# Matmuls on a constant tile, placed in TensorE's early waits, in a linear-attention kernel with a feed-forward block

## The chip, the cores and the metric

The kernel runs on one core of a Trainium2 chip. A core has a matrix engine (TensorE, PE in the profile, with its weight loads shown as PEld), a vector engine (VectorE, DVE), a scalar engine (ScalarE, ACT), a general engine (GpSimd, POOL) and an engine that mainly issues transfers (SyncE, SP). SBUF is the on-chip memory that the engines work in; PSUM holds the results of matmuls, here in eight banks. Each engine takes its instructions in order, and they wait for one another by semaphores.

The metric is the device time of one execution in microseconds. The number given for a kernel is the median of its runs.

## The reference

For 8 batches of 8 heads, with 576 rows of 64 elements, the attention part computes a kernelized attention with 128 random features; its output, 4608 rows of 512, goes through a feed-forward block of 2048 hidden elements.

```python
def phi(x):
    proj = np.einsum('bhsd,md->bhsm', x, omega)
    sq = np.sum(x * x, axis=-1, keepdims=True) / 2.0
    h = proj - sq
    h = h - np.max(h, axis=-1, keepdims=True)
    return np.exp(h) / np.sqrt(m)
q_p, k_p = (phi(q_s), phi(k_s))            # q and k scaled by 64 ** -0.25
kv = np.einsum('bhsm,bhsd->bhmd', k_p, v)
z = np.sum(k_p, axis=2)
num = np.einsum('bhsm,bhmd->bhsd', q_p, kv)
den = np.einsum('bhsm,bhm->bhs', q_p, z)[..., None] + 1e-06
x = (num / den)                            # to rows of 8 heads * 64
h = x @ w_in
g = h * np.clip(h + 3.0, 0.0, 6.0) / 6.0
out = g @ w_out
```

The constants of `phi` that depend on a row alone cancel between numerator and denominator for q; for k the maximum is divided out of v (`cc`, the reciprocal of `mx`).

## The kernel before

The program is written as a list of operations, and a planner in the kernel's own code puts them in order when the program is built. Each operation (`op`) has the engines that may run it, a cost in microseconds, a priority (lower goes first), the keys that it reads and writes, and, for a matmul, the PSUM bank that it needs (`alloc`; the eight banks are the `ring`, and a `Virt` is a bank not yet chosen). `Prog.schedule` (L102) keeps one clock for each engine. In each step it looks, for every engine, at the operations whose predecessors have been placed, takes the one that can start first (or a more urgent one that can start almost as soon), and over all engines places the earliest. A matmul takes the bank that has been free longest; `slot_of` finds it. Transfers share a modelled bandwidth (`flow`). `Prog.emit` then writes each engine's instructions in the order found, with a semaphore wait wherever an operation depends on one of another engine that is not yet known to be done. The order is thus fixed at build time; only the waits are decided on the chip.

The work of a batch is `attention(b)`:

- `load` brings q, k and v. For batch 0, SP and ACT issue float32 transfers (L467), which are cast on the chip (`cast`, evicted through the helper at L389 to L393). From batch 1 on, POOL issues q and k with a cast in the transfer.
- `turns` transposes k and q on PE (L405 for batch 0, L406 later) and copies the result to `kT` and `qT`.
- The K matmuls (L606) multiply with omega, 128 by 256 columns each, two to an operation; ACT exponentiates them to `kp` (L612) and DVE takes the maximum (L615). `project` does the same for q (L623 on PE, L627 on ACT).
- `pair` makes, for two heads, `cc` (L707), the scaled v (`vc`, L711 and L716), the product kv (L724, L726), its copy `kvz`, the numerators (L747), the division (L759, L763) and the transposition of the result to `xT` (`turn_x`). Batch 0 does this in two halves, "A" and "B".

The feed-forward block of a batch follows one batch behind: `mm1_half` (L840) for batch 0, in two halves of 256 rows, `mm1` (L815) later, and `mm2` (L870) one further behind. Their matmuls are the dense part of the run.

What starts the transfers matters for the change. At the start SP issues omega (L412), k and q, the remaining rows of k, and v. POOL issues the four pieces of w_in (L443) behind the landing of v of batch 0 (`W_GATE`). k of batch 1 waits for the third piece of w_in, q of batch 1 for the fourth:

```python
    W_GATE = [("v32", 0, 1), ("v32", 0, 3), ("v32", 1, 3), ("v32", 1, 3)]
...
            load(1, (), {"k": [("wi", 2)], "q": [("wi", 3)], "v": [("kb", 1, 16)]})
```

The first instructions of PE are one matmul that makes omega's transposed copies (L428, behind two casts on DVE, with two copies by DVE after it, L431 and L433), then the transposes of k of batch 0.

Of the kernel before, what the change touches and what calls it, by code (L numbers as in the profile page):

```python
# [5 lines left out]
BF16 = mybir.dt.bfloat16  # L6
# [4 lines left out]


URGENT = 0.5
EV0 = (("ACT","DVE"), ("ACT","DVE"), ("POOL","DVE"), {"k": ("POOL", "ACT", "DVE"), "q": ("POOL", "ACT","DVE")})


# [24 lines left out]
class Prog:  # L41
# [60 lines left out]
    def schedule(self):  # L102
        for o in self.ops:
            o.ndep = len(o.deps)
            for d in o.deps:
                d.succ.append(o)
        engines = {}
        for o in self.ops:
            for e in o.engs:
                engines.setdefault(e, [])  # L110
        free = {e: 0.75 for e in engines}
        queues = {}
        clock = [0.0]

        def flow(until, keep):

            now, qs = clock[0], {q: [list(x) for x in l] for q, l in queues.items()}
            while True:
                heads = [l for l in qs.values() if l and l[0][2] <= now + 1e-9]
                later = [l[0][2] for l in qs.values() if l and l[0][2] > now + 1e-9]  # L120
                if not heads and not later:
                    break
                if not heads:
                    step = min(later) - now
                    if now + step >= until:
                        break
                    now += step
                    continue
                total = sum(l[0][0].packet for l in heads)
                step = min([l[0][1] * total / l[0][0].packet for l in heads] + [x - now for x in later] +  # L130
                           [until - now])
                now += step
                for l in heads:
                    l[0][1] -= step * l[0][0].packet / total
                    if l[0][1] <= 1e-9:
                        l[0][0].end = now
                        l.pop(0)
                if now >= until - 1e-9:
                    break
            if keep:  # L140
                clock[0] = max(until, clock[0])
                queues.update(qs)

        def ready(o):
            return max(o.ready, max([d.end + d.lat + o.slack for d in o.late])) if o.late else o.ready

        def add(o):
            o.ready = max([d.end + (0.0 if d.eng == "PE" and o.engs == ("PE",) else d.lat + o.slack)
                           for d in o.deps if d.group is None] + [0.0])
            o.late = [d for d in o.deps if d.group is not None]  # L150
            for e in o.engs:
                engines[e].append(o)

        for o in self.ops:
            if o.ndep == 0:
                add(o)
        order = []
        n = len(self.ops)

        def slot_of(o):  # L160
            t, picks = 0.0, []
            for vx in o.alloc:
                idle = sorted((0.0 if h is None else h.free_at, i) for i, h in enumerate(vx.ring.held)
                              if h is None or h.left == 0)
                if len(idle) <= o.spare:
                    return None
                t = max(t, idle[o.spare][0])
                picks.append(idle[0][1])
            return t, picks

        while len(order) < n:
            best = None
            for e, lst in engines.items():
                cand = []
                for o in lst:
                    s = slot_of(o) if o.alloc else (0.0, ())
                    if s is None:
                        continue
                    cand.append((max(free[e], ready(o), s[0]), o, s[1]))
                if not cand:  # L180
                    continue
                m = min(x[0] for x in cand)
                c = min((x for x in cand if x[0] <= m + (URGENT if x[1].prio < -1.0 else 0.02)),
                        key=lambda x: (x[1].prio, x[1].seq))
                if best is None or c[0] < best[0]:
                    best = (c[0], e, c[1], c[2])
            if best is None:
                raise RuntimeError("stuck: " + str([(e, [o.name for o in l][:5]) for e, l in engines.items()]))
            st, e, o, picks = best
            for x in o.engs:  # L190
                engines[x].remove(o)
            o.eng = e
            occ = o.occ[e] if isinstance(o.occ, dict) else o.occ
            for vx, i in zip(o.alloc, picks):
                old = vx.ring.held[i]
                if old is not None:
                    for d in old.users:
                        o.deps.setdefault(d, False)
                vx.slot = i
                vx.ring.held[i] = vx  # L200
            o.start = st
            if o.group is not None:
                free[e] = st + o.issue
                flow(free[e], True)
                queues.setdefault(e, []).append([o, occ, free[e]])
                flow(1e9, False)
            else:
                free[e] = st + occ
                o.end = free[e]
            for vx in o.virts:  # L210
                vx.left -= 1
                vx.free_at = max(vx.free_at, o.end + o.lat)
            order.append(o)
            for s in o.succ:
                s.ndep -= 1
                if s.ndep == 0:
                    add(s)
        self.order = order
        return order
# [79 lines left out]
def _emit(nc, es, q, k, v, omega, w_in, w_out, out):  # L299
# [20 lines left out]
    alpha = float(D) ** -0.25  # L320
    PE_T, PE_X = 2, 2
    SPARE = 1
    EV_T = ("DVE", "ACT")
    EV_C = ("POOL", "ACT", "DVE")
    EV_V = ("POOL", "DVE")
    EV_L = ("POOL", "ACT")
    K0, T0, V0, C0 = EV0
    EV_K = ("DVE", "ACT")
    EV_O = ("ACT", "DVE")

    def sbt(name, shape, dt):
        return es.enter_context(nc.sbuf_tensor(name, list(shape), dt))
# [5 lines left out]
    q32 = sbt("q32", [128, NCH, D], F32)  # L338
# [22 lines left out]
    osb = [sbt("osb%d" % u, [128, HID], F32) for u in range(4)]  # L361
    wi = sbt("wi", [128, NJ, DFF], BF16)
    wo = sbt("wo", [128, NF, HID], BF16)
    om32 = sbt("om32", [M, D], F32)
    om2 = sbt("om2", [M, 2, D], BF16)
    om = sbt("om", [128, 2, M], BF16)
# [4 lines left out]
    ring = Ring([P8[:, i, :] for i in range(8)])  # L371
# [3 lines left out]
    op = G.op  # L375
# [10 lines left out]
    def both(n, fast=1):  # L386
        return {"ACT": actt(n), "DVE": 0.07 + n / 960.0 / fast}
# [36 lines left out]
    for i in range(2):  # L424
        op("DVE", 0.15, lambda E, i=i: E.tensor_copy(om2[:, i, :], om32[:]), -9, reads=["om32"],
           writes=[("om2", i)])
    vom = Virt(ring)
    op("PE", 0.1, lambda E: E.matmul(ring.t[vom.slot][:, 0:M], om2[:].rearrange("m t d -> m (t d)"), ident[:],  # L428
                                     start=True, stop=True),
       -9, reads=[("om2", 0), ("om2", 1), "ident"], writes=[vom], alloc=[vom], lat=0.25)  # L430
    op("DVE", 0.2, lambda E: E.tensor_copy(om[0:64, 0, :], ring.t[vom.slot][0:64, 0:M]), -9, reads=[vom],  # L431
       writes=["om0"])
    op("DVE", 0.2, lambda E: E.tensor_copy(om[64:128, 1, :], ring.t[vom.slot][64:128, 0:M]), -9, reads=[vom],  # L433
       writes=["om1"])
    omk = ["om0", "om1", "omz0", "omz1"]


    WI = [(0, 4), (4, 8), (8, 12), (12, 16)]
# [73 lines left out]
    def attention(b):  # L512
        pb = b % 2
        sl = 0.0 if b == 0 else 1.0
        sp = 0 if b == 0 else SPARE

# [26 lines left out]
        def turns(t, name, dbl, dst, src, p):  # L543
# [3 lines left out]
            def e_T(E):  # L547
# [5 lines left out]
               writes=[vT], alloc=[vT], lat=0.25, slack=sl, spare=sp, name="T%s%d.%s" % (t, b, name))  # L553
            op(EV_T if b else T0, both(n, 1 if b else 2), evac(lambda: dst, lambda: turned(vT, b, n).rearrange(
                "p (j t) -> p j t", j=dst.shape[1])),
# [143 lines left out]
    def pair(b, m, t):  # L699
        pb = b % 2  # L700
        sl = 0.0 if b == 0 else 1.0
        sp = 0 if b == 0 else SPARE
        u2 = (b * NP + m) % 2
# [184 lines left out]
    for b in range(B):  # L888
        if b == 0:
            load(0, ("SP", "ACT", "SP", "ACT"), {t: [] for t in "kqv"})  # L890
            for i in range(len(WI)):
                w_in_piece(i, [W_GATE[i]])
        elif b == 1:
            load(1, (), {"k": [("wi", 2)], "q": [("wi", 3)], "v": [("kb", 1, 16)]})
            for g, key in enumerate((("qb", 1, 16),("qb", 1, 16),("qb", 1, 16),("qb", 1, 16))):
                w_out_piece(g, [key])
        elif b == 2:
            load(2, (), {"k": [("wo", 2)], "q": [("wo", 3)], "v": [("wo", 3)]})
        else:
            load(b, (), {"k": [("m1", b - 2, 6)], "q": [("m1", b - 2, 9)], "v": [("m1", b - 2, 15)]})  # L900
        attention(b)
        if b == 0:
            continue
        blk = b - 1
        if blk == 0:
            for half in range(2):
                for f in range(0, NF, 2):
                    mm1_half(half, f)
            continue
        for f in range(NF):  # L910
            mm1(blk, f)
            if f % 4 == 0:
                mm2(blk - 1, f // 4)
# [47 lines left out]
```

## Time and profile before

| | us |
|---|---|
| median of 5 runs | 331.83 |
| the five runs | 329.91, 331.05, 331.83, 332.25, 332.53 |
| the profiled execution: its time | 330.35 |
| the profiled execution: its span | 328.5 |

A profile is taken of one execution. Its span runs from the first instruction to the last; 1.85 us of that execution's time lie around it.

| engine | busy us | share of the span | instructions |
|---|---|---|---|
| PE | 313.1 | 95% | 2185 |
| DVE | 209.5 | 64% | 455 |
| ACT | 193.6 | 59% | 393 |
| POOL | 77.5 | 24% | 109 |

Busy time is an average over the whole run; the change touches only the first stretch of it. There the engines look as follows (busy time of each engine in stretches from the start of the span):

| stretch, us | PE | DVE | ACT | POOL |
|---|---|---|---|---|
| 5 to 6 | 0.53 | 0.41 | 0.55 | 0.00 |
| 8 to 9 | 1.00 | 1.00 | 0.86 | 0.94 |
| 11 to 12 | 0.97 | 0.42 | 1.00 | 0.60 |
| 12 to 13 | 0.26 | 1.00 | 1.00 | 0.79 |
| 13 to 14 | 0.26 | 0.97 | 1.00 | 0.93 |
| 15 to 16 | 0.53 | 0.97 | 0.48 | 0.87 |
| 18 to 19 | 0.70 | 0.91 | 0.78 | 0.70 |
| 22 to 23 | 1.00 | 0.06 | 0.36 | 0.00 |
| 29 to 30 | 0.21 | 1.00 | 0.92 | 0.68 |
| 30 to 31 | 0.40 | 0.70 | 0.00 | 0.00 |

PE waits longest, in order of time, before its first matmul (3.37 us), before the first transposes of k (1.82 us, at 5.47), before the q projections (1.48 us, at 13.74, for ACT's copy of qT), before the first kv (0.64 us, at 15.47), and before the transposes of k of batch 1 at 30.07. In the profile, "idle before" is the time for which an engine had nothing running ahead of an instruction, and the name behind the arrow is what released it. The ends of matmuls are modelled, and matmuls overlap, so the rate of PE is better read from start to start of many equal ones than from the length of one.

### The profile page before, as it was taken

Reading aid. Unit: us, or ns where it says so; the run is one execution under the profiler, and the core shown is the slowest. Engines: PE = TensorE matmul, PEld = TensorE weight load, DVE = VectorE, ACT = ScalarE, POOL = GpSimd, SP = SyncE. Lnnn points to the kernel's source line nnn. Section 1 sums busy time; section 2 is a strip of 40 time slices with the busy share of each in tenths; the row PEclk is TensorE's granted clock in tenths of the full one; section 3 lists DMA queues with packets and bytes.
Section 4 is the critical chain, followed back from the end, with each engine's and each line's share of the span. In section 5 each row is a group of like instructions: output and inputs, shape, how many; then the busy total and the mean of one; then the engine's idle time right before and its main releaser. Section 6 shows DMA issues by size and latency. Waiting matters only on the chain.

```text
span 328.5 us, 5726 instructions
## 1 busy us (share of the span) xinstructions
PE 313.1 (95%) x2185; PEld 168.6 (51%) x2185; DVE 209.5 (64%) x455; ACT 193.6 (59%) x393; POOL 77.5 (24%) x109
## 2 busy tenths in 40 slices
PE   3788999999999999999999999999999999999994
PEld 2466774555545554555555555555555444444442
DVE  4868896599777757875687577856775433443311
ACT  3877992389369546764776477646764444344400
POOL 2815527037034402240235023502110000000000
PEclk9999999999999999999999999999999999999999
DMA  7999999969993996799569963997022111000033
GB/s 257 240 184 149 228 181 144 254 167 154 208 199 44 161 198 193 89 159 188 191 79 148 190 208 38 154 210 225 10 56 60 39 50 48 33 32 34 34 86 72
DMA packets 89355, 44.32 MB, mean 135 GB/s; under 512 B 56048, under 2 KB 84720, under 8 KB 89328
## 3 DMA queue, kind: packets, MB, share of 16 engines
q1 hardware_dynamic: 62272, 30.98, 40.7%
q0 software_dynamic: 26512, 12.46, 31.2%
q10 hardware_dynamic: 544, 0.52, 0.5%
q8 instruction: 17, 0.28, 0.4%
q14 instruction: 10, 0.08, 0.1%
HBM read 36.73 MB, written 9.44 MB: 141 GB/s over the span
## 4 chain that ended last, share of the span: by engine, by line
PE 86%; DMA 8%; POOL 1%; ACT 1%; issue 1%; SPq 1%; DVE 0%; POOLq 0%
PE p L870 37%; PE p L815 34%; PE p L623 4%; PE p L606 3%; DMA wi<-in_moe_w_in_dram 3%; PE p L747 3%; PE p L724 2%; DMA xT<-xb 2%; PE p L840 2%; DMA q<-in_q_dram 2%; DMA k<-in_k_dram 1%; PE p L406 1%; SPq L467 1%; POOL wi L443 1%; PE p L726 0%
## 5 line engine op out<-in xcount | busy, mean ns | idle before, releaser
L870 PE MATMUL p<-wo,gT 128*128 128x512 bf16 x576 | 142.8, 379 | 0.0
L823 DVE SCALAR_TENSOR_TENSOR gT<-tsb,p 128x512 bf16<-128x512 bf16 x128 | 87.4, 686 | 68.0 <-ACT tsb L821 67.6
L821 ACT ACTIVATE tsb<-p 128x512 bf16<-128x512 f32 x128 | 76.8, 602 | 69.6 <-PE p L815 68.3
L815 PE MATMUL p<-xT,wi 128*128 128x512 bf16 x448 | 111.6, 379 | 0.5 <-DMA xT<-xb 0.5
L870 PEld LDWEIGHTS p<-wo,gT 128*128 128x128 bf16 x576 | 55.3, 98 | 55.9
L815 PEld LDWEIGHTS p<-xT,wi 128*128 128x128 bf16 x448 | 42.9, 98 | 46.3 <-DMA xT<-xb 1.0
L612 ACT ACTIVATE kp<-p 128x512 bf16<-128x512 f32 x72 | 42.1, 609 | 24.7 <-PE p L606 24.4
L615 DVE TENSOR_REDUCE mx<-kp 128x4 f32<-128x512 bf16 x72 | 47.9, 678 | 11.4 <-ACT kp L612 11.0
L627 ACT ACTIVATE qpT<-p 128x512 bf16<-128x512 f32 (+1 forms) x80 | 43.1, 570 | 4.4 <-PE p L623 4.4
L711 POOL TENSOR_TENSOR vc<-v,cc 128x512 bf16<-128x512 f32 x24 | 25.1, 1047 | 46.9 <-DVE cc L707 26.8
L763 DVE TENSOR_TENSOR xb<-p,rec 128x384 bf16<-128x384 f32 (+1 forms) x64 | 28.4, 477 | 0.0
L606 PE MATMUL p<-om,kT 128*128 128x256 bf16 x144 | 26.5, 285 | 0.1
L623 PE MATMUL p<-qT,om 128*128 128x512 bf16 (+1 forms) x80 | 25.1, 358 | 1.5 <-ACT qT L392 1.5
L392 ACT COPY osb<-p 128x512 f32<-128x512 f32 x30 | 17.6, 588 | 6.7 <-PE p L870 6.3
L606 PEld LDWEIGHTS p<-om,kT 128*128 128x128 bf16 x144 | 13.5, 101 | 10.6 <-DVE kT L393 0.7
L646 POOL TENSOR_TENSOR vcl<-vl,cc 64x260 bf16<-64x260 f32 x6 | 3.7, 616 | 60.8 <-DMA vl<-in_v_dram 35.1
L747 PEld LDWEIGHTS p<-kvz,qpT 128*128 128x128 bf16 x312 | 13.9, 98 | 7.2 <-DVE kvz L393 0.6
L815 PE MATMUL p<-xS,wi 128*128 128x512 bf16 x64 | 16.4, 379 | 0.0
L840 PE MATMUL p<-xT,wi 128*128 128x256 bf16 x128 | 15.6, 273 | 0.2 <-ACT xT L392 0.2
L724 PEld LDWEIGHTS p<-vc,kp 128*128 128x128 bf16 x256 | 11.8, 98 | 7.8 <-DVE vcl L646 1.1
L747 PE MATMUL p<-kvz,qpT 128*128 128x65 bf16 x312 | 15.3, 194 | 0.6 <-DVE kvz L393 0.3
L724 PE MATMUL p<-vc,kp 128*128 128x65 bf16 x256 | 13.5, 194 | 1.6 <-DVE vcl L646 0.6
(71 smaller groups left out, 200.2 us busy)
## 6 DMA issues: line engine op xcount, KB each, us to landing
out_dram<-osb SPq DMA_DIRECT2D x32, 256.0 KB, 3.7
v<-in_v_dram SPq DMA_DIRECT2D x14, 512.0 KB, 5.4
wi<-in_moe_w_in_dram POOLq DMA_DIRECT2D x4, 512.0 KB, 9.3
k<-in_k_dram POOLq DMA_DIRECT2D x8, 256.0 KB, 4.5
k<-in_q_dram POOLq DMA_DIRECT2D x8, 256.0 KB, 5.6
wo<-in_moe_w_out_dram POOLq DMA_DIRECT2D x4, 512.0 KB, 10.1
kb<-in_k_dram POOLq DMA_DIRECT2D x6, 256.0 KB, 4.4
qb<-in_q_dram POOLq DMA_DIRECT2D x6, 256.0 KB, 7.2
```

Of the source, the lines that this page charges most:

```text
L606: ins = E.matmul(ring.t[vK.slot][:, 256 * i:256 * i + 256], kT[:, 2 * u + i, :], om[:].rearrange("d t m -> d (t m)"), start=True, stop=True)
L612: op("ACT", actt(512), lambda E, u=u, vK=vK: E.activation(kp[pb][:, 4 * u:4 * u + 4, :].rearrange("p c m -> p (c m)"), ring.t[vK.slot], AF ...
L615: op("DVE", dvet(512), lambda E, u=u: E.reduce_max(mx[pb][:, 4 * u:4 * u + 4], kp[pb][:, 4 * u:4 * u + 4, :], axis=AX.X), pos(u) + 0.03, r ...
L623: op("PE", mmt(n), lambda E, vQ=vQ, lh=lh: E.matmul(ring.t[vQ.slot][:, 0:n], om[:, lh, :], src, start=True, stop=True), p + 0.045 * lh, re ...
L627: op("ACT", actt(n), lambda E, vQ=vQ, lh=lh: E.activation(dst(lh), ring.t[vQ.slot][:, 0:n].rearrange("m (j t) -> m j t", t=128), AF.Exp, s ...
L724: E.matmul(o[:, 65 * hh:65 * hh + 65], kp[pb][:, c0 + i, :], vc[u2][:, 65 * i:65 * i + 65], start=(i == 0), stop=False)
L747: ins = E.matmul(d[:, hh, i - i0, :], qpT[pb][:, o:o + 128], kvz[m][:, 65 * hh:65 * hh + 65], start=True, stop=True)
L763: op("DVE", dvet(128 * n), lambda E: E.tensor_tensor(xv[:, :, i0:i1, :], psum()[:, :, :, 0:64], rbc, ALU.mult), t + 0.01, reads=[vn, ("rec ...
L815: ins = E.matmul(ring.t[vh.slot], wi[:, c, 128 * f:128 * f + 128], xv[:, c, :], start=(c == 0), stop=(c == NJ - 1))
L821: op("ACT", actt(512), lambda E: E.activation(tsb[tu][:], ring.t[vh.slot], AF.Relu, bias=0.5, scale=1.0 / 6.0), t - 0.1, reads=[vh], write ...
L823: op("DVE", dvet(512), lambda E: E.scalar_tensor_tensor(gT[gu][:, f, :], tsb[tu][:], 1.0, ring.t[vh.slot], ALU.min, ALU.mult), t - 0.1, re ...
L870: ins = E.matmul(ring.t[vo.slot], gT[gu][:, f, 128 * tc:128 * tc + 128], wo[:, f, :], start=(f == 0), stop=(f == NF - 1))
```

## The change

A tile `fill` of 128 by 384 bf16 is set to one by DVE at the start. Forty operations named "idle" are added for PE, each one matmul of 128 columns of `fill` (the weights) on 256 others. Each takes a PSUM bank; nobody reads what it writes. Sixteen of them depend on `fill` alone and have a cost of 0.22 us in the plan; 24 also depend on the last of q's main rows of batch 0 and have a cost of 0.11 us. They have the lowest priority, and the planner treats them apart: it takes the first idle operation only if it would end before the earliest other operation that PE could start, and only up to 21 us of its clock. When nothing but idle operations is left, the planner stops, and any that were not placed are not written.

```diff
+IDLE_UNTIL = 21.0
...
-                m = min(x[0] for x in cand)
+                idle = [x for x in cand if x[1].name == "idle"]
+                cand = [x for x in cand if x[1].name != "idle"]
+                m = min([x[0] for x in cand] + [1e9])
+                if idle and (not cand or idle[0][0] + idle[0][1].occ <= m):
+                    if idle[0][0] > IDLE_UNTIL:
+                        if not cand:
+                            continue
+                    elif best is None or idle[0][0] < best[0]:
+                        best = (idle[0][0], e, idle[0][1], idle[0][2])
+                        continue
+                    else:
+                        continue
+                if not cand:
+                    continue
...
+            if best is None and all(o.name == "idle" for l in engines.values() for o in l):
+                break
...
+    IDLE = (16, 24)
...
+    fill = sbt("fill", [128, 384], BF16)
...
+    op("DVE", 0.2, lambda E: E.memset(fill[:], 1.0), -9.5, writes=["fill"])
+
+    def idle_work(count, each, gate):
+        for i in range(count):
+            vw = Virt(ring)
+            op("PE", each, lambda E, vw=vw: E.matmul(ring.t[vw.slot][:, 0:256], fill[:, 0:128], fill[:, 128:384],
+                                                     start=True, stop=True),
+               9, reads=["fill"] + gate, writes=[vw], alloc=[vw], lat=0.0, name="idle")
...
+        if b == 0:
+            idle_work(IDLE[0], 0.22, [])
+            idle_work(IDLE[1], 0.11, [("q32", 1, 3)])
         attention(b)
```

## The prediction

> **What bounds the kernel now.** First the page: PE is busy 313.1 of 328.5 us, and the chain of waits is 86% PE. So a gain must either shorten PE's dense work or let it start sooner. The change adds 40 matmuls and removes none, so only the second is open. Next the waits of PE over the whole span: of 10.8 us, all but 1.1 us (0.55 at 50.19 us, 0.49 at 94.81 us) lie before 33.1 us. The question is thus what ends the early waits, and PE's timeline there shows it (columns: start, us, engine, line, operation, tiles, count, idle before with releaser):
>
> ```profile
> 5.47 1.03 PE L405 MATMUL p<-ident,kb 128*128 128x128 bf16 x8 [1.82 <-DVE kb L393]
> ...
> 8.28 1.91 PE L606 MATMUL p<-om,kT 128*128 128x256 bf16 x8
> 9.99 0.63 PE L405 MATMUL p<-ident,qb 128*128 128x128 bf16 x4
> 10.41 0.32 PE L405 MATMUL p<-ident,kb 128*128 128x128 bf16 x2
> 10.57 1.02 PE L606 MATMUL p<-om,kT 128*128 128x256 bf16 x6
> 11.43 0.83 PE L405 MATMUL p<-ident,qb 128*128 128x128 bf16 x12
> ...
> 30.07 0.40 PE L406 MATMUL p<-ident,k 128*128 128x128 bf16 x4 [0.85 <-DMA k<-in_k_dram]
> 31.01 0.27 PE L406 MATMUL p<-ident,k 128*128 128x128 bf16 x2 [0.55 <-DMA k<-in_k_dram]
> ```
>
> The last two rows are the point of this case: PE has finished all it can do for batch 0 and stands 0.85 + 0.55 = 1.40 us for k of batch 1. The chain of waits, asked for 0 to 36 us, says why k comes no sooner (start, us, what):
>
> ```profile
> 13.76 10.42 DMA wi<-in_moe_w_in_dram
> 24.18 0.29 issue
> 24.47 1.53 POOL k L467 x2
> 26.00 4.88 DMA k<-in_k_dram
> 30.88 0.14 issue
> 31.01 0.29 PE p L406 x2
> ```
>
> No PE work stands in it from 0 to 31 us. k of batch 1 is issued by POOL when the third piece of w_in (L443) has landed, those pieces when v of batch 0 has landed, and v when SP has worked through its queue. The second finding is a slow start of PE. The instructions of L606 from 5 to 9 us, and from 10.9 to 11.5 us (ns min/median/max):
>
> ```profile
> L606 PE MATMUL p<-om,kT x8: 394/421/421, 6.6 to 8.9; 128*128 128x256 bf16 x8
> ```
> ```profile
> L606 PE MATMUL p<-om,kT x5: 272/273/283, 10.7 to 11.3; 128*128 128x256 bf16 x5
> ```
>
> The same matmul falls from 421 to 273 ns at about 10.5 us, although the row of granted clock reads 1.00 in every microsecond from 0 to 34. Start to start it is (1.91 - 0.421)/7 = 0.213 us early and, from the 42 matmuls of L840 in 4.75 us at 21.57, (4.75 - 0.273)/41 = 0.109 us later. PE runs at half rate up to 10.5 us, and full from then on: the 65-column matmuls of L724 and L747 show 192 to 204 ns throughout 15 to 20 us.
>
> **The change part by part.** *The constant tile.* One DVE memset of 128x384 bf16. Between the 64x64 memset (0.11 us) and the 128x260 uint32 one (0.28), both rows of DVE; I take the upper, as the size in bytes is nearer to it. DVE idles 1.33 us before omega's cast at 3.01, so it costs nothing; without that cover, 0.28.
>
> *Where the 40 fillers go.* A filler is planned only where it ends before PE's next known work, so the order of the real work is kept. The planner's clock, worked from the costs in the code, agrees with the trace (k's transposes 30.01 planned, 30.07 measured); I use it only to place them. The first 16, at 0.22 each: 12 ahead of omega's matmul (planned 1.15 to 3.79), 4 behind it. The 24 gated on q (planned landing 9.17; the last casts of q start on the chip at 9.31 after a landing at 9.04): 2 behind q's first transposes, 2 ahead of the last K matmuls, 10 in the wait for qT (13.74, 1.48 us), 6 ahead of the first kv (15.47, 0.64 us), 3 and 1 in the next two waits (0.25 and 0.28 us).
>
> *Cost of the first 16.* 12 x 0.213 = 2.56 us from about 1.1 us on (DVE's first memset starts at 0.81, plus 0.28): they end near 3.7, and omega's matmul moves from 3.37 to 3.7. Its two copies (3.69 to 4.28) move 0.3 us into DVE's idle 0.70 us ahead of 4.99. The other 4 take 0.85 us, to 4.9 at the latest, inside the wait that k's cast ends at 5.47. Sum 0. Gone the cover, it would be 0.3 us at the first K matmul.
>
> *What they bring.* PE is now active from 1.1 us instead of 5.47. If it is at full rate by 7 us, the work from 7.43 to 10.5 takes half. What is late next is ACT: its idle after 7 us is only 0.24 us before 7.24, some 0.14 us around 8.8 and 0.24 us ahead of 10.77, then it is full to 15.2. From above: at full rate already at 5.47, the first exponential (ACT, idle 1.17 us before 7.24) comes about 0.5 us sooner too. So the batch-0 chain comes forward 0.4 to 0.9 us at most.
>
> *Cost of the 24.* Two and two go where the trace has no gap (9.99 to 12.2 is solid): 4 x 0.109 = 0.44 us, or 0.85 at half rate. The 10, the 6 and the 4 need 1.09, 0.65 and 0.44 us against waits of 1.48, 0.64 and 0.53: hidden within 0.01. A filler also waits for the readers of the PSUM bank it takes; no row shows such waits. Between 0 (the bank planned free is free; it can't be a gain) and the whole next wait, I take 0, since all banks around 12.7 to 13.8 are freed by ACT's exponentials (trace: done at 13.20), ahead of the qT copies that PE awaits there anyway.
>
> *Sum.* At the first mm1 (20.79) between 0.9 us sooner and 0.44 later. Either way it runs into the 1.40 us wait for k at 30.88. Does PE reach the chain that lands k? One place: POOL's `vc` (L716, 12.35) stands in its queue between the first and second w_in issue, and hangs on cc, done by DVE at 10.21. That is 2.1 us of slack, and before cc only the first 16 fillers stand. So k stays, and behind it ACT (kT, xT, qpT in a row from 31.32) and PE keep their order; 0.21 us of PE's wait at 33.07 (ACT xT, queued behind kT) can't move much. Sum on the profiled execution: 328.5 of span + 1.85 around it = 330.35, change -0.1, within +-0.3. The runs' median lies 1.48 above that execution. I carry the -0.1 to the median: **331.7 us**.
>
> **A rule weighed.** The Trainium skill, TensorE: Matmul & The Clock Gate, Part 1, says that half rate is the default, that about 3.4 us of sustained work lifts it, counted in a free-running window. Trace: 5.47 to 10.5 is 5.0 us. By its penalty rule (time throttled times one half) 5.0/2 = 2.5 us are to be had: 329.3. By the trace, where the time goes into the 1.40 us wait, nothing: 331.7. The measured wait decides. Against the 24, the same page ("HAM oscillation") has the clock fall only after a PE gap of over some 3.4 us; the longest wait after 5.47 here is 1.48 us, and the trace indeed shows no second fall. By this rule the 24 protect nothing; but it also lets the phase differ from run to run, which one trace can't exclude.
>
> **The rivals.** *A: no change* as above, 331.7. Chance 0.52.
>
> *B: the median run is slower than the profiled one because its clock rises late or falls again.* PE is busy only 26% from 12 to 14 us and about half in 15 to 17. Half rate over 32 matmuls of mm1 (3.4 us) adds 32 x 0.104 = 3.3 us; less the slack of 1.40 it leaves 1.9, just what lies between the lowest run (329.91) and the median. The fillers then bring the median to about **330.0** (330.35 and 329.91 are what good executions show). For it: five runs spread over 2.6 us. Against: the one trace shows no such fall, and transfers vary too. Chance 0.28.
>
> *C: the fillers overrun the waits.* PE takes them in order; if the array stays at half rate among them, 24 x 0.213 = 5.1 us stand in waits of 1.48 + 0.64 + 0.53 = 2.65, 2.45 too long; less 1.40 that the wait for k takes up, +1.1: **332.9**. At each one's whole 421 ns, with nothing overlapped, 10.1 - 2.65 - 1.40 = +6.1: 337.9, the upper end. I price it by the start-to-start row. It decides from 1.40 us of delay on. Against: L840's spacing shows full rate at that time. Chance 0.20.
>
> *D: the fillers don't lift the clock*, since constants might not count as activity: nothing moves at the end, so D is within A.
>
> **How the numbers follow.** I call 0.5% (1.7 us) what a measurement of this kernel can tell from no change. A: 0.02 faster, 0.47 same, 0.03 slower, for the spread of medians. B: 0.23 faster, 0.05 same (330.0 is 0.55% down, close to the bound). C: 0.11 slower by its upper part, 0.09 same. Sums: 0.25, 0.61, 0.14. A's own range is 330.9 to 332.5 (the spread of medians). The range goes down to 329.8 for all of B but an edge, and up to 333.5, which takes the lower half of C; what is left out is C's upper half (0.10) and edges of the others.
>
> **What would show it.** Right: L606 at 273 ns well before 10.5 us, mm1's first matmul moved by under 1 us, and PE's wait for k at 30 us longer by just as much, with k still landing near 30.9. A fall of 421 ns rows that reaches the end would need k to land sooner, which would make me wrong. C shows as mm1 starting after 22.2 us and no wait left before k's transposes; a changed moment of the w_in issues would break the argument at its root. B can't be seen in one trace, only in the spread of the runs: it would fall below that of before.

## The result, and the profile after

| | before | after |
|---|---|---|
| median of all runs taken side by side, us | 330.66 (79 runs) | 330.07 (44 runs) |
| lowest to highest, us | 328.59 to 333.75 | 328.86 to 333.03 |
| profiled execution: time and span, us | 330.35 and 328.5 | 329.53 and 327.7 |

The ratio after to before is 0.999, with a 95% interval of 0.9977 to 1.0004: no change that can be told from none. The median of before that the prediction started from (331.83, 5 runs) was a high draw of the same kernel.

The head of the page after shows the 40 added matmuls, with a weight load each, and the one added memset:

```profile
span 327.7 us, 5807 instructions
...
PE 316.9 (97%) x2225; PEld 171.1 (52%) x2225; DVE 209.5 (64%) x456; ACT 193.5 (59%) x393; POOL 77.4 (24%) x109
```

PE is busy 3.8 us more in a span 0.8 us shorter. In PE's timeline of the changed kernel (start, us, engine, line, operation, tiles, count, idle before with releaser; the lines of the file have moved, so that L423 is the old L405, L424 the old L406, L634 the old L606, L752 the old L724 and L868 the old L840) the added matmuls are L461:

```profile
1.32 2.74 PE L461 MATMUL p<-fill 128*128 128x256 bf16 x12 [1.32 <-DVE fill L456]
3.86 0.31 PE L446 MATMUL p<-ident,om 128*128 128x128 bf16 x1
3.96 0.80 PE L461 MATMUL p<-fill 128*128 128x256 bf16 x4
5.40 0.62 PE L423 MATMUL p<-ident,kb 128*128 128x128 bf16 x8 [0.64 <-DVE kb L411]
...
10.59 0.28 PE L423 MATMUL p<-ident,kb 128*128 128x128 bf16 x2 [1.37 <-DVE kb L411]
...
12.24 1.61 PE L461 MATMUL p<-fill 128*128 128x256 bf16 x10
...
14.81 0.82 PE L461 MATMUL p<-fill 128*128 128x256 bf16 x6
...
21.25 0.83 PE L868 MATMUL p<-xT,wi 128*128 128x256 bf16 x6
...
29.51 0.39 PE L424 MATMUL p<-ident,k 128*128 128x128 bf16 x4
31.23 0.27 PE L424 MATMUL p<-ident,k 128*128 128x128 bf16 x2 [1.33 <-DVE gT L879]
```

Three things are to be seen. The clock rises early: the eight transposes at 5.40 take 0.62 us, 1.03 before. What that wins is lost at 10.59, where PE waits 1.37 us for the cast of the remaining rows of k; these landed at 10.2 us, and the fillers don't hasten a landing. And the wait ahead of k's transposes at 31 us, put down to k's landing before, is now put down to DVE's `gT`. The chain of waits after, from 0 to 36 us, has it too:

```profile
30.57 0.60 DVE gT L879
```

But the releaser is inferred, and here it is the wrong one. The transfers of the changed kernel (tile, queue, count, size, us from issue to landing) show when the last rows of k landed:

```profile
k<-in_k_dram POOLq DMA_DIRECT2D x1, 64.0 KB, 5.7
```

They were issued at 25.41, so they landed at 31.1 us and the transposes followed 0.1 us later, just as before (30.88 and 31.01). That this `gT` ended at 31.17 is a coincidence: in a run below whose engines work in the same order (k sooner, all 40), the same six transposes start at 29.11 and are done before it starts. DVE's timeline there:

```profile
30.09 0.68 DVE L879 SCALAR_TENSOR_TENSOR gT<-tsb,p 128x512 bf16<-128x512 bf16 x1
```

So PE waits for k before and after. Batch 0 itself hangs on the landing of v, which came 0.4 us later in this execution. DVE's first scaled v and the first mm1, before:

```profile
11.93 0.69 DVE L711 TENSOR_TENSOR vc<-v,cc 128x512 bf16<-128x512 f32 x1 [0.58 <-DMA v<-in_v_dram]
20.79 0.83 PE L840 MATMUL p<-xT,wi 128*128 128x256 bf16 x6
```

and the scaled v after (the mm1 is in the timeline above, at 21.25):

```profile
12.35 0.69 DVE L739 TENSOR_TENSOR vc<-v,cc 128x512 bf16<-128x512 f32 x1 [0.56 <-DMA v<-in_v_dram]
```

Measured from that scaled v, which takes the landing out, the first mm1 comes 8.86 us later before and 8.90 after. The 40 matmuls neither shorten nor lengthen batch 0 in these two executions.

### The profile page after: what moved, and what is told of

The parts are those of the page before. It is cut to its first block, busy times and chain, and to the rows that moved or that the text cites. A ratio compares the mean times of both kernels' runs of the same rounds, so it can differ in the third digit from the quotient of the medians.

```text
span 327.7 us, 5807 instructions
## 1 busy us (share of the span) xinstructions
PE 316.9 (97%) x2225; PEld 171.1 (52%) x2225; DVE 209.5 (64%) x456; ACT 193.5 (59%) x393; POOL 77.4 (24%) x109
## 4 chain that ended last, share of the span: by engine, by line
PE 91%; DMA 3%; DVE 2%; SPq 2%; ACT 1%; issue 0%; DVEq 0%
PE p L898 37%; PE p L843 34%; PE p L651 4%; PE p L868 4%; PE p L634 4%; PE p L775 3%; PE p L752 3%; SPq L495 2%; DMA xT<-xb 2%; DMA v<-in_v_dram 2%; PE p L424 1%; DVE mx L643 1%; PE p L754 1%; PE p L688 0%; PE p L423 0%
## 5 line engine op out<-in xcount | busy, mean ns | idle before, releaser
L634 PE MATMUL p<-om,kT 128*128 128x256 bf16 x144 | 25.5, 273 | 0.6 <-DVE kT L411 0.3
L634 PEld LDWEIGHTS p<-om,kT 128*128 128x128 bf16 x144 | 13.0, 98 | 10.8 <-ACT kT L410 0.8
L868 PE MATMUL p<-xT,wi 128*128 128x256 bf16 x128 | 15.7, 273 | 0.2 <-ACT xT L410 0.2
L752 PEld LDWEIGHTS p<-vc,kp 128*128 128x128 bf16 x256 | 11.9, 98 | 6.2 <-DVE vcl L674 0.6
L752 PE MATMUL p<-vc,kp 128*128 128x65 bf16 x256 | 13.5, 194 | 0.3 <-DVE vcl L674 0.3
```

Of the source, the lines that this page charges most:

```text
L634: ins = E.matmul(ring.t[vK.slot][:, 256 * i:256 * i + 256], kT[:, 2 * u + i, :], om[:].rearrange("d t m -> d (t m)"), start=True, stop=True)
L752: E.matmul(o[:, 65 * hh:65 * hh + 65], kp[pb][:, c0 + i, :], vc[u2][:, 65 * i:65 * i + 65], start=(i == 0), stop=False)
L868: ins = E.matmul(ring.t[vh.slot][:, 256 * g:256 * g + 256], wi[:, c, 128 * (f + g):128 * (f + g) + 128], xT[0][:, c, 256 * half:256 * half ...
```

## The experiments

One column of the tables below is new: every execution lists the mean granted clock over its span, and it falls into groups. Of 152 executions of the kernel before, taken beside the runs below, 90 have 0.984 to 0.992, 18 have 0.993 to 0.996, and 40 have 0.999 or 1.000 (4 lie between). The profiled execution of before belongs to the last group.

**One half of the change at a time.** `IDLE = (16, 24)` becomes

```diff
-    IDLE = (16, 24)
+    IDLE = (16, 0)
```

in the first kernel and `(0, 24)` in the second.

> Only the 16 matmuls ahead of k's landing, without the 24 in the attention. Theory (the clock is lifted, but the end is set by landings): the 256-column matmuls of K show 273 ns from the first on (421 in the kernel before until 10.5 us), and the first mm1 still starts 8.8 to 9.0 us after DVE's first scaled v (8.86 before, 8.90 with all 40); time 0.997 to 1.003 of before. Rival (these 16 bring something and the 24 take it back): the first mm1 starts under 8.5 us after that, time under 0.997. Rival (the clock falls again in the attention without the 24): 421 ns matmuls after 12 us, time above 1.003.

> Only the 24 matmuls behind q's landing, without the 16. Theory: K's matmuls are at 421 ns until about 10.5 us as in the kernel before, since nothing stands before 9 us; the first mm1 8.8 to 9.2 us after DVE's first scaled v (the four that stand between K's matmuls cost at most 0.4); time 0.997 to 1.003. Rival (the 24 overrun their waits): the first mm1 more than 9.3 us after, time above 1.003.

| | ratio to before (95%) | executions at a clock of 0.992 or less |
|---|---|---|
| 16 early alone | 0.9985 (0.9965 to 1.0004) | 16 of 22 |
| 24 late alone | 0.9996 (0.9969 to 1.0023) | 0 of 14 |
| all 40 | 0.999 (0.9977 to 1.0004) | 0 of 44 |
| none (before) | | 90 of 152 |

The times tell nothing apart, the clocks do. With the early 16 alone, PE by stretches (from:to, length, PE busy and instructions, granted clock, transfers) shows the clock at half from about 18 to 25 us:

```profile
12.00:16.00 4.00, 1.55 (x16) 1.00 0.94 167
16.00:20.00 4.00, 3.09 (x52) 0.78 1.11 167
20.00:24.00 4.00, 3.83 (x22) 0.50 1.24 206
24.00:28.00 4.00, 4.00 (x34) 0.87 1.09 149
```

The same stretches of the changed kernel:

```profile
12.00:16.00 4.00, 3.57 (x30) 1.00 0.96 170
16.00:20.00 4.00, 3.66 (x62) 1.00 1.17 176
20.00:24.00 4.00, 3.85 (x37) 1.00 1.24 205
24.00:28.00 4.00, 4.00 (x43) 1.00 1.06 144
```

PE is busy only 1.55 us of the 4 ahead of the fall, with no wait over 1.48 us, and the clock falls all the same; with the fillers it is busy 3.57 us and the clock stays. In halves of a microsecond the clock is at 0.50 from 18.5 to 25.0 us with the 16 alone. Half rate over 6.8 us of a 328.6 us span gives a mean of 1 - 0.5 x 6.8/328.6 = 0.990, which is this execution's mean; that is how the group at 0.992 or less is to be read. (No execution of the kernel before that falls was profiled; the runs below without the late 24 were, and show the same fall.) The first mm1 came 9.53 us after the scaled v instead of 8.86, and the end of the first half of mm1 (the transposes of xb ahead of k's) 19.22 us after it instead of 16.90: the fall costs batch 0 2.3 us here (1.7 and 1.3 in two traces further down). Yet the span is 328.6 us, against 328.5 before. Most of the delay goes into the wait for k: the last two transposes that await it start at 31.82 in this trace, with no wait, against 31.01 before. So without the fall k's landing sets the time of these transposes; with it batch 0 does, some 0.8 us later.

The rival of the first run, a clock that falls without the 24, had the mechanism right and the time wrong. In the second run the fillers didn't overrun their waits: 8.85 us from the scaled v to mm1.

**How much lateness the end forgives.** The kernel before with extra matmuls directly ahead of the first mm1:

```diff
             def e(E, a0=a0, a1=a1):
+                if half == 0 and f == 0 and a0 == 0:
+                    for _ in range(13):
+                        E.matmul(ring.t[vh.slot][:, 0:256], ident[:], om[:].rearrange("d t m -> d (t m)"),
+                                 start=True, stop=True)
```

> The kernel before with 13 extra matmuls of 256 columns (1.42 us at full rate) directly ahead of the first mm1, so that the batch-0 work of PE is late by that. Prediction's reading (1.40 us of slack ahead of k's transposes): end unchanged, 331 +-0.5, ratio 0.998 to 1.003; the second group of k's transposes starts within 0.3 us of k's landing. Rival (the slack is only some 0.2 us, since those transposes also wait for DVE to read a PSUM bank, which ended 0.18 us before k landed): they start about 1.2 us after k's landing, released by DVE, and the ratio is 1.002 to 1.005.

> The same with 39 extra matmuls (4.25 us). Prediction's reading: 4.25 - 1.40 = +2.85 us, ratio about 1.009. Rival (slack 0.2): +4.05 us, ratio about 1.012. If the later dense stretch takes some back (PE waits after 36 us were 1.04 us in the trace of before), each is up to 1 us less.

Measured: 1.002 (0.9998 to 1.0041) with 13, 1.0124 (1.0077 to 1.0172, 6 runs) with 39, which is +0.7 and +4.1 us. This can't tell a slack of 1.40 from 0.2, because the dose was not the intended one. In both traces the clock had fallen by then (at 0.992 or less: 15 of 22 and 5 of 6 executions), and the extra matmuls began at half rate: scaled v to first mm1 took 11.96 us (11.85 to 23.81) and 14.58 us (13.64 to 28.22), so 3.1 and 5.7 us late, against an execution of before without the fall, instead of 1.42 and 4.25. The 27 executions of before with the fall in this series average 330.80 us, the 16 at 0.999 or more 330.25; those with the fall average 331.68 with 13 and 335.20 with 39. So a delay of 1.3 to 2.3 us (the fall alone) costs 0.6 us, one of 3.1 us costs 1.4 and one of 5.7 us costs 5.0, with standard errors of 0.4 to 0.5: between 0.7 and 1.7 us are forgiven. As a number the slack stays rough. But the rival's reason for a small one, that the transposes also wait for DVE, is out: in the trace with 13 the six run in one piece from 32.06 and are done by 32.6, and the `gT` in question starts at 33.03. That so much lateness reaches the end is shown.

**Moving k.** The landing of k is moved by its gate: sooner with

```diff
-            load(1, (), {"k": [("wi", 2)], "q": [("wi", 3)], "v": [("kb", 1, 16)]})
+            load(1, (), {"k": [("wi", 1)], "q": [("wi", 2)], "v": [("kb", 1, 16)]})
```

once without and once with the 40 matmuls, and later with `("wi", 3)` for k.

> The kernel before with k of batch 1 gated on the second piece of w_in instead of the third, and q on the third instead of the fourth, so that they are issued some 2 us sooner and fill the transfers' idle stretch at 25 to 26.3 us. Theory (two chains end within 0.5 us of each other at 31 us: w_in to k's landing, and v's landing through batch 0 to the PSUM bank that k's transposes take): k lands 1 to 2 us sooner, but its second group of transposes starts only 0.1 to 0.5 us sooner, released by DVE; ratio 0.997 to 1.001. Rival (k's landing alone sets the end): they start 1.3 us sooner or more and the ratio is 0.995 to 0.997. Half of the executions still show a mean granted clock of 0.992 or less.

> The same gates with the 40 matmuls on the constant tile. Theory: with k out of the way, the batch-0 chain sets the end, and the clock's fall in it counts in full: no execution at a clock of 0.992 or less, and 0.3 to 1.0 us under the same kernel without the 40; ratio to before 0.994 to 0.998. Rival (the fall costs nothing even then): equal to the kernel without the 40 within 0.3 us.

> The kernel before with k of batch 1 gated on the last piece of w_in (about 1 us later). Theory: k's landing and the transposes move by 0.5 to 1.5 us, and the end by 0.3 to 1.2 us, since PE's later waits (1.04 us in the trace of before) take some back; ratio 1.001 to 1.004. Rival (the end doesn't hang on k's landing): ratio within 0.999 to 1.001. The fall of the clock changes nothing here.

| | ratio to before (95%) | clock 0.992 or less |
|---|---|---|
| k sooner, no fillers | 0.9979 (0.996 to 0.9998) | 15 of 22 |
| k sooner, all 40 | 0.9929 (0.9913 to 0.9945) | 1 of 22 |
| k later, no fillers | 1.0045 (1.0014 to 1.0077) | 6 of 9 |

This decides. k's landing does bound the changed kernel: with k sooner, the same 40 go from 0.999 to 0.9929. In the kernel before it isn't the only bound: moved out of the way, it brings 0.7 us. And the same 40 matmuls that are worth nothing at the old gate bring 1.4 us more at the new one (medians 329.68 and 328.31). The fall is a part of that: in the kernel without fillers the 15 executions with the fall average 330.07 us, the 7 others 329.27. The step from there to the 328.38 with all 40 is 0.9 us with a standard error of 0.4, and is not explained.

The run with k later tells less than it seems to (+1.5 us, beyond what I expected). There the planner also changed the order of the engines' work: in its trace eight matmuls of mm1 stand ahead of k's transposes, which start 1.5 us after k's landing (33.9) without waiting for it:

```profile
35.42 0.94 PE L406 MATMUL p<-ident,k 128*128 128x128 bf16 x14
```

What a later landing costs by itself isn't shown. The other gates leave the order of PE's work as it was.

PE's timeline with k sooner and the 40 has no wait for k left:

```profile
28.89 0.39 PE L423 MATMUL p<-ident,xb 128*128 128x128 bf16 x4
29.11 0.50 PE L424 MATMUL p<-ident,k 128*128 128x128 bf16 x6
```

The six transposes of k run in one piece right behind batch 0's; the last two start at 29.34, 1.7 us ahead of where they stood before (31.01). Without the fillers the six start at 30.81, behind a batch 0 that is late by the fall (9.90 us from scaled v to mm1). I had expected DVE to release them there; in the trace they follow batch 0's last work without a wait. Its ratio came out as expected, the reason was another.

**Which of the 40, and how far.** The halves again at the sooner gate, and the gate one piece sooner still (`("wi", 0)` for k, `("wi", 1)` for q).

> k and q of batch 1 gated one piece of w_in sooner, with only the 24 late matmuls. Theory (the gain is that the clock doesn't fall in the attention): no execution of a clock of 0.992 or less, the first mm1 8.8 to 9.0 us after DVE's first scaled v, ratio to before 0.992 to 0.995, as with all 40 (0.9929). Rival (the early 16 bring the gain, or a part): 0.996 to 0.999.

> The same gates with only the 16 early matmuls. Theory: two thirds of the executions at a clock of 0.992 or less, time as with the gates alone (0.9979): 0.996 to 0.999. Rival (the early 16 bring the gain): 0.992 to 0.995.

> All 40, with k gated on the first piece of w_in and q on the second: one piece sooner still. Theory: k already lands before PE wants it, so nothing is left to gain there; k's bytes now stand among those of w_in and the third and fourth piece land later, so PE waits for w_in in mm1: ratio to before 0.993 to 0.998, no better than the 0.9929 of one piece sooner. Rival (the wait for k is still in the way in part of the executions): under 0.992.

| k sooner, with | ratio to before (95%) | clock 0.992 or less | scaled v to first mm1, us | to the end of its first half, us |
|---|---|---|---|---|
| 24 late | 0.9944 (0.992 to 0.9968) | 0 of 19 | 8.82 | 16.86 |
| 16 early | 0.9989 (0.9966 to 1.0012) | 19 of 22 | 9.87 | 18.57 |
| all 40 | 0.9929 (0.9913 to 0.9945) | 1 of 22 | 9.00 | 17.04 |
| all 40, one more piece sooner | 0.9943 (0.9916 to 0.997) | 2 of 15 | 9.10 | 17.14 |

The 24 late ones bring the gain; the 16 early ones lift the clock and bring nothing that shows. With the 16 alone, the 19 executions with the fall average 330.08 us and the 3 without 328.82, close to the 328.70 of the late 24: here the fall is nearly the whole difference, as far as 3 executions can tell. The stretches with the 16 alone show where the time goes (same columns as above):

```profile
16.00:18.00 2.00, 1.12 (x15) 0.85 1.18 180
18.00:20.00 2.00, 1.68 (x26) 0.50 1.22 192
20.00:22.00 2.00, 1.82 (x24) 0.50 1.23 208
22.00:24.00 2.00, 2.00 (x10) 0.50 1.25 204
24.00:26.00 2.00, 2.00 (x20) 0.94 1.27 195
```

PE is full from 22 us on, in mm1, and runs at half rate: ten matmuls from 22 to 24, twenty from 24 to 26. One more piece sooner gains nothing further, but that edit moved the issue of k and not its landing: the last rows landed 17.3 us after the scaled v in both traces. The wait for w_in that I expected there did not appear.

**Where the executions at 0.993 to 0.996 come from.** They are the longest of the changed kernel (13 of 44; mean 331.35 us, against 329.76 at 0.999 and above). I suspected the wait ahead of k's transposes and filled it with ten more matmuls, as an operation of cost zero in the plan:

```diff
+            op("PE", 0.0, e_hold, 0.02, reads=["fill", ("xb", 0, 0, 1), ("xb", 0, 1, 1)], writes=[vh0],
+               alloc=[vh0], lat=0.0, name="hold")
```

> The changed kernel with 10 more matmuls on the constant tile (1.09 us) behind the last work of batch 0 that PE has before k's transposes, where PE waits 0.85 to 1.6 us. Asked: whether the executions of the changed kernel at a mean clock of 0.994 to 0.996 (13 of 44, mean 331.35 us against 329.76 us at 0.9985 and above) come from a fall of the clock in that wait. If so, none is left at 0.996 or less and the median falls by some 0.4 us (ratio to before 0.997 to 0.999). If not, about 3 in 10 are still there, and the time is the changed kernel's or up to 0.5 us more (ratio 0.998 to 1.001).

Measured: 1.0001 (0.997 to 1.0033), and 2 of 14 executions still at 0.993 and 0.994, of 331.64 and 333.64 us. The suspicion is wrong, and the profiled execution, one of those two, shows the real place. First PE's timeline of it, then stretches of its clock (from:to, length, PE busy and instructions, granted clock, transfers):

```profile
8.57 1.04 PE L423 MATMUL p<-ident,kb 128*128 128x128 bf16 x8 [1.63 <-POOL kb L411]
```

```profile
7.50:8.00 0.50, 0.00 (x0) 0.89 1.09 376
8.00:8.50 0.50, 0.00 (x0) 0.50 1.18 319
...
11.00:11.50 0.50, 0.50 (x6) 0.70 1.04 329
```

k of batch 0 came late, PE stood 1.63 us for its cast, and the clock was at half from 7.9 to 11.2 us, 3.4 us. The scaled v started only at 13.73 us. In this execution the fall and the longer time have one cause, late transfers at the start; one trace, so that this holds for the whole group is likely but not shown. Why the group is larger in the changed kernel (13 of 44) than before (18 of 152) is open.

## Why the prediction was right, and where its steps were not

*The size.* Forecast: -0.1 us, no change. Measured: 0.999, which is -0.3 us with -0.8 to +0.1 allowed. The wait for k does what the forecast said; that the number is so close is in part luck, since the forecast has no fall of the clock in it, and the gain at batch 0 that the wait was to swallow never came.

*The constant tile and the first 16.* Right in effect. The memset took 0.38 us, not 0.28 (the time goes with the elements, not the bytes: 0.11, 0.28 and 0.38 us for 64, 260 and 384 in a row); omega's matmul moved to 3.86 us, 0.5 us later instead of 0.3, and its copies to 4.21, still ahead of the cast at 4.92. The clock rose within the four fillers at 3.96 us (421 to 273 ns), so D, constants that don't count, is out.

*The places of the 24.* Wrong in one point: none stands among the K matmuls. They are 10, 6, 3, 4 and 1, all in waits. The 0.44 us that the sum had for four of them was not there.

*0.4 to 0.9 us sooner.* Missed: it was zero in these two executions. I had ACT as what is late next; it was the landing of the remaining rows of k (1.37 us of wait at 10.59) and then of v, from which the rest of batch 0 hangs.

*The 1.40 us of slack ahead of k.* Right in kind: it is a wait for k, and delays of batch 0 go into it, 0.7 to 1.7 us of them by the runs above. PE's later waits (1.04 us before, 0.3 in the changed kernel) may give part of a delay back as well; how much isn't shown.

*"The trace shows no second fall".* True of the trace, false of the kernel: 90 of 152 executions have it. I drew a fixed property from one execution and leaned on the rule for support. The Trainium skill's page TensorE: Matmul & The Clock Gate ("HAM oscillation") lets the clock fall after PE gaps of over some 3.4 us; here it fell with none over 1.48 us, at a busy share of 1.55 in 4 us, so the measurement decides against the rule as I used it. Its Part 1, a window that runs free of the kernel, fits that only some executions show the fall.

*Rival B* had the mechanism and was mis-sized. Its fall is real, of 6.8 us rather than 3.4, and the late 24 remove it. Its price was to be 3.3 us at batch 0 and, less 1.40, 1.9 us at the end. Batch 0 is late by 1.3 to 2.3 us in the traces that have it; executions of before with the fall average 330.62 (standard error 0.12) and those at 0.999 or more 330.09 (0.20), so it is 0.5 at the end. Times the share of 90 in 152 that makes 0.3 us, as much as the change measures, though that measure is not clear of none. More of the price comes out when k is moved: there the early 16 alone (19 of 22 with the fall) average 329.91 us and the late 24 alone (none) 328.70, 1.2 us apart.

*Rival C*, fillers that overrun their waits, didn't occur: 8.82 to 9.10 us from scaled v to mm1 in every kernel with the late 24.

## What to carry to other kernels

A clock that one trace shows at full rate may fall in half of the executions: look at the mean clock of all of them before saying what a filler can bring. Where two chains end together, a remedy for one is worth nothing until the other is moved, and a change that measures as nothing may be half of one that pays (0.999 and 0.9979 alone, 0.9929 together). A releaser in a profile is inferred: when a transfer lands and an engine ends at nearly the same moment (31.1 and 31.17 here), look for a run in which the two are apart before building on the name. And a gate that is moved can move more than the landing: compare the order of work and the landing itself.

## What was not expected of the hardware

The granted clock fell to 0.50 without any long wait, with PE busy 1.55 us in 4, and came back only 6.8 us later although PE was busy 3.83 of the 4 us from 20 to 24. Conversely, the row of granted clock reads 1.00 in the first 10 us of the kernel before, while its matmuls last 421 ns instead of 273: for the start, the length of equal matmuls is the better witness. A tile of ones is enough to lift the clock: the sixteen begin at 1.32 us, with one other matmul among them, the fourteenth takes 364 ns at 4.18 us, and the last two 273 ns.
